# Moving the first loads, the narrowing of weights and the odd output tile of a fused FNet and gated-FFN kernel

## The chip, the cores and the metric

One NeuronCore of one Trainium2 chip runs the whole program. The metric is the device time of one execution in microseconds (us), given as the median of several runs with the lowest and highest beside it. A profile is one such execution seen by the hardware profiler; its span is some 2 us shorter than the time. The engines are called PE (TensorE matmul), PEld (its weight load), DVE (VectorE), ACT (ScalarE), POOL (GpSimd) and SP (SyncE, which here only issues transfers).

## The reference, cut to what matters

```python
X = np.fft.fft(np.fft.fft(x, axis=1), axis=2).real      # x: (8, 3136, 256) float32
h = np.maximum(X @ w_in, 0)                             # w_in: (256, 1024)  float64
c = sum(conv_w[k] * pad(h)[:, k:k + S] for k in range(3))  # three taps along the sequence
out = ((h / (1 + np.exp(-c))) @ w_out).astype(np.float32)  # w_out: (1024, 256) float64
```

The weights come as float64, so the kernel has to make float32 of their bit patterns itself, which is called narrowing here.

## The kernel before

For each of the 8 batches, DVE folds x (it uses the symmetries of the transform along the sequence, 14 operations per batch), PE multiplies the folds with tables of sines and cosines (the Fourier stage, nine *units* per batch), and then 32 *steps* follow: four *chunks* of the sequence times eight blocks of 128 features. In a step, PE makes two products (`pb`, `pa`), ACT copies one of them (`nb`), DVE adds and subtracts them with a clamp at zero (two "clamp adds", which make the front and the mirrored back part of `h`), ACT and DVE apply the three taps, ACT the sigmoid, POOL and DVE the gate, and three steps later PE multiplies the block with its part of `w_out`. The folds and units of the next batch are laid out as extra work into the steps of the batch before. Only batch 0 has to do its stage with nothing else to run.

The start: the order in which transfers are issued, and the tiny transfers of one partition each.

```python
w_cv.load(nc.scalar)
w_in[0].load(nc.scalar, 0)
w_in[0].load(nc.sync, 1)
for h in range(2):
    for f in load_ops(0, h, nc.sync):   # plain x, [five zero rows if h], 4 mirrored (indirect)
        f()
nc.scalar.dma_start(out=dm, in_=dft_dim[:, :, 0:2])
load_tables(1)                          # two big transfers and two table rows
for t in range(2):
    w_in[1].load(nc.sync, t)
load_tables(0)
...
w_cv.narrow(0, slice(0, P))
for t in range(2):
    w_in[0].narrow(t, slice(0, H))      # 7 DVE operations each
for f in fold_ops(0):
    f()
w_out.load(nc.sync)
taps()
blocks(0)                               # products of w_in's first half with dft_dim
for par in (1, 0):
    mend_tables(par, half)              # ACT: a halved row; for par 1 also two signed tables
```

The Fourier stage of batch 0, with a quarter of w_in's second half narrowed in each of four units, and what goes into the first steps:

```python
quarters = [(t, slice(i * H // 2, (i + 1) * H // 2)) for t in range(2) for i in range(2)]
for i, u in enumerate(us[j] for j in (0, 1, 4, 2, 3, 5, 6, 7, 8)):
    u.matmuls(0, 1)
    u.copy()
    ...
    u.fin()
    ...
    if i in (0, 1, 4, 5):
        w_in[1].narrow(*quarters.pop(0))
...
at(0, "pe", lambda: blocks(1))
for c in range(NF):
    at(c, "dve", lambda c=c: w_out.narrow(c, slice(0, D)))
```

The last product and the way out. A chunk has six tiles of 128 rows (one of them in a batch has 127), the last one seven, of which the seventh has 65 rows.

```python
osp = ctx.enter_context(tc.tile_pool(name="osp", bufs=3))
...
mm(pt[0:m, i % 2, :], gs[s][:, o:o + m], wout[:, f, :], ...)
if f == NF - 1 and (i % 2 or i == len(tiles) - 1):
    osb = osp.tile([P, 2, D], F32, name="os", tag="os")
    for j in range(i - i % 2, i + 1):
        nc.scalar.copy(out=osb[0:m, j % 2], in_=pt[0:m, j % 2])
        nc.sync.dma_start(out=rows[b * S + r:b * S + r + m, :], in_=osb[0:m, j % 2])
```

## Time and profile before

The time is 1279.84 us (1279.60 to 1280.65, three runs). I cut the span into the stretches that have different limits, by the times of the first clamp add of each batch:

| stretch | from to (us) | limit |
|---|---|---|
| loads, until PE starts the Fourier stage | 0 to 51.5 | transfers |
| stage of batch 0 | 51.5 to 73.3 | PE, then DVE |
| batch 0 | 73.3 to 248.0 | DVE in its first 19 steps |
| batches 1 to 5 | 248.0 to 992.3 | DVE and PE, in turns |
| batches 6 and 7 | 992.3 to 1276.1 | PE |
| last copy to the end | 1276.1 to 1279.0 | output transfers |

The page, the chain, SP's timeline and the busy times by stretch are shown in the prediction.

### The profile page before, as it was taken

To read this page: it belongs to the slowest core of one execution; us is meant where nothing else is said; L and a number is where in the kernel's file an instruction comes from. 1 tells how busy PE (TensorE), PEld (TensorE's weight loads), DVE (VectorE), ACT (ScalarE), POOL (GpSimd) and SP (SyncE) were. 2 spreads that over 40 slices of the span, in tenths; PEclk is the share of its full clock that TensorE was granted. 3 is DMA by queue.
4 is the path that set the end of the run, shared out by engine and by line. 5 is a ranking of instruction groups with operands and counts; after the bars stand their busy time and mean duration, and the time that the engine had idled before them with its cause. 6 is when DMAs were issued, how large, how long until landed. Compare 5 with 4: busy or idle time off the path is not lost.

```text
span 1279.0 us, 15442 instructions
## 1 busy us (share of the span) xinstructions
PE 1196.6 (94%) x4914; PEld 898.0 (70%) x4914; DVE 1145.5 (90%) x1689; ACT 884.4 (69%) x1823; POOL 398.5 (31%) x500
## 2 busy tenths in 40 slices
PE   2487899999999999999999999999999999999998
PEld 1355677677777777777677777777777777777776
DVE  7399999999999898998999888998999888898996
ACT  0254666677767777777777777777777777778885
POOL 4112532434424133241424224241322213222222
PEclk8688999999999999999999999999999999999999
DMA  7421321111212012020202103020010001000001
GB/s 198 122 76 33 94 76 47 55 52 52 68 59 76 11 43 76 25 78 25 89 13 63 41 25 101 26 78 5 22 50 26 27 26 44 32 17 15 26 29 44
DMA packets 47098, 66.04 MB, mean 52 GB/s; under 512 B 5600, under 2 KB 35196, under 8 KB 47016
## 3 DMA queue, kind: packets, MB, share of 16 engines
q1 hardware_dynamic: 41444, 51.39, 13.0%
q0 software_dynamic: 5120, 12.85, 3.6%
q10 hardware_dynamic: 452, 0.81, 0.2%
q8 instruction: 38, 0.62, 0.2%
q14 instruction: 44, 0.36, 0.1%
HBM read 39.24 MB, written 25.74 MB: 51 GB/s over the span
## 4 chain that ended last, share of the span: by engine, by line
PE 66%; DVE 16%; DMA 6%; issue 5%; ACT 5%; POOL 2%; SPq 1%; DVEq 0%; ACTq 0%; POOLq 0%
PE po L90 41%; PE pb L90 10%; PE pa L90 9%; PE pd L90 7%; DVE g L517 4%; DVE h L505 2%; DVE g L531 2%; DMA xh<-in_x_dram 2%; ACT nb L494 2%; DMA tab<-dft_seq_dram 2%; DMA out_dram<-os 2%; DVE xh L151 1%; ACT g L523 1%; DVE xh L162 1%; POOL xh L126 1%
## 5 line engine op out<-in xcount | busy, mean ns | idle before, releaser
L90 PE MATMUL po<-wout,g 128*128 128x256 f32 (+2 forms) x3200 | 742.4, 382 | 29.2 <-DVE g L531 25.7
L90 PEld LDWEIGHTS po<-wout,g 128*128 128x128 f32 (+2 forms) x3200 | 599.2, 188 | 193.9 <-DVE g L531 58.0
L517 DVE SCALAR_TENSOR_TENSOR g<-h,cw,g 128x770 f32<-128x770 f32 (+2 forms) x512 | 556.1, 1086 | 11.0 <-ACT g L511 1.5
L530 POOL TENSOR_TENSOR g<-g,h 128x385 f32<-128x385 f32 (+1 forms) x256 | 243.9, 954 | 760.6 <-ACT g L523 569.2
L523 ACT ACTIVATE g<-g 128x385 f32<-128x385 f32 (+3 forms) x512 | 244.0, 527 | 209.7 <-DVE g L517 209.5
L494 ACT ACTIVATE nb<-pb 128x386 f32<-128x386 f32 (+4 forms) x512 | 225.5, 493 | 98.0 <-PE pb L90 97.4
L505 DVE CUSTOM_DVE_ANT_0 h<-pa,nb 128x386 f32<-128x386 f32 (+4 forms) x512 | 264.8, 559 | 1.7 <-PE pa L90 1.6
L511 ACT ACTIVATE g<-h,cw 128x770 f32<-128x770 f32 (+2 forms) x256 | 243.5, 951 | 0.0
L90 PE MATMUL pb<-qt,G 127*128 127x386 f32 (+2 forms) x512 | 215.4, 501 | 4.8 <-ACT nb L494 4.8
L90 PE MATMUL pa<-pt,G 128*128 128x386 f32 (+2 forms) x512 | 213.3, 497 | 2.7 <-DVE pt L262 2.7
L531 DVE TENSOR_TENSOR g<-g,h 128x385 f32<-128x385 f32 (+2 forms) x256 | 154.6, 604 | 9.9 <-ACT g L523 9.9
L479 ACT ACTIVATE pa<-eb,ge 128x386 f32<-128x386 f32 (+2 forms) x256 | 153.6, 600 | 0.0
L90 PEld LDWEIGHTS pa<-pt,G 128*128 128x128 f32 x512 | 97.4, 190 | 77.1 <-issue 23.4
L90 PE MATMUL pd<-tab,w 99*128 99x196 f32 (+2 forms) x448 | 117.8, 374 | 0.0
L90 PEld LDWEIGHTS pb<-qt,G 127*128 127x128 f32 x512 | 94.2, 191 | 30.7 <-ACT nb L494 6.4
L126 POOL DMA_INDIRECT xh<-in_x_dram,idx x64 | 96.4, 1506 | 18.1 <-issue 12.0
L90 PEld LDWEIGHTS pd<-tab,w 99*128 99x128 f32 (+1 forms) x448 | 83.0, 190 | 13.6
L547 ACT COPY os<-po 128x256 f32<-128x256 f32 (+2 forms) x200 | 60.0, 395 | 23.3 <-DMA out_dram<-os 16.2
L151 DVE TENSOR_TENSOR xh<-xh 98x1020 f32<-98x1020 f32 (+1 forms) x32 | 44.9, 1409 | 0.0
L90 PE MATMUL po<-tab,w 98*128 98x196 f32 (+4 forms) x64 | 16.6, 420 | 26.3 <-ACT tab L215 15.6
L162 DVE TENSOR_TENSOR xh<-xh 98x1024 f32<-98x1024 f32 (+1 forms) x32 | 40.8, 1275 | 0.1
L90 PEld LDWEIGHTS po<-tab,w 98*128 98x128 f32 (+1 forms) x64 | 12.8, 215 | 29.6 <-ACT tab L215 16.1
(90 smaller groups left out, 324.5 us busy)
## 6 DMA issues: line engine op xcount, KB each, us to landing
out_dram<-os SPq DMA_DIRECT2D x184, 128.0 KB
xh<-in_x_dram SPq DMA_DIRECT2D x16, 784.0 KB
eb<-ed SPq DMA_DIRECT2D x16, 193.0 KB
tab<-dft_seq_dram SPq DMA_DIRECT2D x4, 601.8 KB
raw<-in_moe_w_out_dram SPq DMA_DIRECT2D x1, 2048.0 KB
eb<-ed SPq DMA_DIRECT2D x8, 209.0 KB
eb<-ed SPq DMA_DIRECT2D x8, 192.5 KB
raw<-in_moe_w_in_dram SPq DMA_DIRECT2D x3, 512.0 KB
```

The costliest lines, as they stand in the source:

```text
L90: nc.tensor.matmul(o, l, r, start=start, stop=stop, skip_group_check=True)
L126: nc.gpsimd.indirect_dma_start(out=xh[b, h][0:NP, 4 + m].rearrange("p q d -> p (q d)"), out_offset=None, in_=bass.AP(tensor=x.tensor, offs ...
L151: vt(a[:, :, :, 1:D], a[:, :, :, 1:D], r[:, :, :, D - 1:0:-1], op=ALU.add)
L479: act(pa[s][:, 0:n], eb[b, c], AF.Copy, scale=ge[:, f:f + 1])
L494: act(nb[s][:, i, cols], p[:, cols], AF.Copy, scale=-1.0 if i else 1.0)
L505: nc.vector._custom_dve(TENSOR_ADD_SAT, out=to, in0=a[:, cols], in1=c[:, i, cols], s0=BIG, s1=0.0)
L511: act(gs[s], hs[s][:, 0:n], AF.Copy, scale=cw[:, 0, s[2]:s[2] + 1])
L517: stt(out=g, in0=h[:, k:k + n], scalar=cw[:, k, f:f + 1], in1=g, op0=ALU.mult, op1=ALU.add)
L523: act(gs[s][:, c], gs[s][:, c], AF.Sigmoid)
L530: gt(g[:, m:n], g[:, m:n], h[:, m + 1:n + 1], op=ALU.mult)
L531: vt(g[:, 0:m], g[:, 0:m], h[:, 1:m + 1], op=ALU.mult)
L547: nc.scalar.copy(out=osb[0:m, j % 2], in_=pt[0:m, j % 2])
```

## The change

Its intent: (1) load x and the first tables ahead of the weights and in fewer transfers; (2) fold batch 0's x ahead of narrowing, and narrow and multiply w_in's first half inside the Fourier stage; (3) narrow w_in's second half in steps 0 and 1; (4) join the 64 odd rows of two batches to one full tile, so that two batches need 49 tiles of the last product and not 50; (5) spread the one-column "feature" products over four column tiles of PE. The core of the diff:

```diff
-            for s0, n, r, d in ((0, 4, 0, Q4), (4, 1, 0, Q4), (5, 1, 3, Q4), (6, 1, 2, Q4), (7, 1, 1, Q4)):
+            for s0, n, r in ((0, 4, 0), (4, 3, 1), (7, 1, 0)):          # zero rows
...
-        nc.sync.dma_start(out=tab[NP:KR, st, HQ - 1], in_=dft_seq[NP:KR, st, 1])
-        nc.sync.dma_start(out=tab[NP:KR, st, 0:HQ - 1], in_=dft_seq[NP:KR, st, 2:HQ + 1])
+    def load_row0():                                                    # one for both pairs
+        nc.sync.dma_start(out=tab[NP:KR, 0:4] ..., in_=...)
...
-    w_in[0].load(nc.scalar, 0)
-    w_in[0].load(nc.sync, 1)
-    for h in range(2):
-        for f in load_ops(0, h, nc.sync):
-            f()
     nc.scalar.dma_start(out=dm, in_=dft_dim[:, :, 0:2])
+    for f in load_ops(0, 0, nc.sync):
+        f()
+    ops = load_ops(0, 1, nc.sync)
+    for f in ops[0:1] + ops[2:]:
+        f()
     load_tables(1)
-    for t in range(2):
-        w_in[1].load(nc.sync, t)
-    load_tables(0)
+    load_row0()
+    ops[1]()                                                            # the zero rows
+    for i in range(2):
+        w_in[i].load(nc.sync)
+        if i == 0:
+            load_tables(0)
...
     w_cv.narrow(0, slice(0, P))
-    for t in range(2):
-        w_in[0].narrow(t, slice(0, H))
...
-    blocks(0)
...
+        if i < 2:
+            w_in[0].narrow(i, slice(0, H))                              # in the stage
-        if i in (0, 1, 4, 5):
-            w_in[1].narrow(*quarters.pop(0))
+        if i == 6:
+            blocks(0)
...
-    at(0, "pe", lambda: blocks(1))
+    for i in range(4):
+        at(i // 2, "dve", lambda i=i: w_in[1].narrow(i // 2, slice(...)))
+    at(1, "pe", lambda: blocks(1))
     for c in range(NF):
-        at(c, "dve", lambda c=c: w_out.narrow(c, slice(0, D)))
+        at(1 + c, "dve", lambda c=c: w_out.narrow(c, slice(0, D)))
...
-    end = 4
+    end = 5
-        stop = per * (b - 1) + max(26 - 8 * b, 2)
+        stop = per * (b - 1) + max(27 - 8 * b, 2)
...
+        if r.start < r.stop:                                            # gate, last chunk
+            vt(left[:, f, b % 2 * LEFT:(b % 2 + 1) * LEFT], g[:, r], h[:, r], op=ALU.mult)
...
+        if ch.last and b % 2:                                           # last product
+            tiles.append((left[:, f], [(i * LEFT, b - 1 + i, ch.rest[1], LEFT) for i in range(2)]))
...
-                        mms.append(product((slice(32 * c, 32 * c + 1), slice(j * n, (j + 1) * n)), ...))
+                        o = 32 * (2 * j + c)                            # feature products
+                        mms.append(product((slice(o, o + 1), slice(0, n)), ...))
```

Also the cuts of the chunks move by a column, the pool of copies gets four buffers, and `eb` four instead of five, with its last chunk loaded a little later.

## The prediction

> **What bounds the kernel now.** I read the page first, then the chain that ended last in order of time, the SP queue's timeline, the stretches of the first 50 us, and the busy time of each engine by step.
>
> From the page, part 1, the TensorE and VectorE rows of part 2, and the head of part 4:
>
> ```profile
> PE 1196.6 (94%) x4914; PEld 898.0 (70%) x4914; DVE 1145.5 (90%) x1689; ACT 884.4 (69%) x1823; POOL 398.5 (31%) x500
> ...
> PE   2487899999999999999999999999999999999998
> ...
> DVE  7399999999999898998999888998999888898996
> ...
> PE 66%; DVE 16%; DMA 6%; issue 5%; ACT 5%; POOL 2%; SPq 1%; DVEq 0%; ACTq 0%; POOLq 0%
> ```
>
> TensorE is full from about 180 us, but not in the first five slices, and the chain is 16% DVE and 6% DMA. So there are three regimes. The chain in order of time gives the first:
>
> ```profile
> 1.70 18.66 DMA xh<-in_x_dram
> ...
> 25.88 22.21 DMA tab<-dft_seq_dram
> 48.24 3.24 ACT tab L215 x4
> 51.52 2.34 PE po L90 x6
> ```
>
> (Start, length, piece.) The first Fourier products (51.5 us) wait for ACT to make two signed tables, and that waits for the second pair of table loads, landed at 48.2 us. Those were issued only at 25 us, because SP stood still before:
>
> ```profile
> 2.15 18.79 SPq L120 DMA_DIRECT2D xh<-in_x_dram  x5
> 20.98 1.67 SPq L202 DMA_DIRECT2D tab<-dft_seq_dram  x2
> ```
>
> The five tiny row transfers take SP 18.8 us: the third to fifth wait for the semaphores of w_in's half and of both big x loads. What that costs shows in the stretches (last column GB/s, before it the DMA share):
>
> ```profile
> 6.00:10.00 4.00, 0.44 (x2) 0.32 (x2) 0.00 (x0) 0.18 (x1) 3.02 (x4) 1.00 1.05 292
> ...
> 19.00:22.50 3.50, 3.50 (x8) 1.49 (x6) 3.43 (x6) 0.59 (x1) 0.68 (x1) 1.00 0.09 23
> 22.50:25.00 2.50, 1.73 (x17) 1.65 (x15) 2.47 (x4) 0.75 (x2) 0.64 (x2) 0.94 0.44 131
> ...
> 40.00:45.00 5.00, 0.00 (x0) 0.00 (x0) 0.00 (x0) 0.00 (x0) 0.00 (x0) 0.50 1.05 224
> ```
>
> 3.5 us with almost no traffic, then a weak 2.5 us. DVE is idle from 35.6 to 54.2 us.
>
> Second regime, batch 0's Fourier stage and the first 19 steps (a step: from one pair of L505 to the next). From 51.5 to 68.6 us TensorE has no gap (17.1 us). After the first L505 at 73.3 us, steps 1 to 18 are DVE without a gap: 7.2 us where a step carries narrowing (2.6) and a fold operation (1.2) besides its own 3.4, about 4.6 with the fold alone.
>
> Third, the steady state, batch 6 (992 to 1135 us) and batch 3 (546 to 695 us):
>
> ```profile
> 992.30:1135.10 142.80, 142.80 (x601) 109.36 (x600) 120.23 (x178) 108.81 (x227) 33.34 (x44) 1.00 0.09 29
> 545.50:694.90 149.40, 146.66 (x610) 110.45 (x608) 136.59 (x200) 109.45 (x227) 49.88 (x61) 1.00 0.16 49
> ```
>
> (Length, then busy PE, PEld, DVE, ACT, POOL.) Batch 6, which folds no later batch, is 100% TensorE. Batch 3, with 17.6 us of folds, takes 6.6 us more: there DVE and TensorE hold each other up step by step.
>
> [...] 22.5 to 25 us, with tables nearly alone, has share 0.44, which is 7/16. [...] The feature products (one output column) use two tiles now; in batch 0 their 16 instructions take 1.57 us [...].
>
> **Part 1, the start.** Removed: two tiny transfers per half-batch and two table-row transfers; the tables no longer queue behind them. In the changed program's instruction stream the SP order is x, x, first tables, rows, zero rows (two with waits), w_in half 0, second tables, w_in half 1, w_out. ACT's signed tables still wait for the second tables, so that landing stays the gate. [...] I take 39.5: **-8.7 us**. The zero rows now queue behind the first tables, so the second half's fold starts near 22 to 26 us and ends by 31 to 35, still earlier than the gate.
>
> **Part 2, batch 0's Fourier stage.** TensorE: 17.1 us as now, plus w_in half 0's products (G, ge), which ran at 18 to 24 us beside idle time and now stand inside the stage: at full clock 74.9 to 81.0 for the other half, 5.5 us. The feature products give back some 0.3. DVE: four quarters of w_in (4 x 2.6 = 10.4) leave, two halves (2 x 4.0 = 7.9) come in; it has 14 us of work under 22.3 of TensorE. So TensorE becomes the bound: 22.3 + 0.33 copy + 0.9 of sums, the first pa product at 23.4 us after the stage's start instead of 20.5: **+2.9 us**. First L505 near 67.5 us.
>
> **Part 3, w_in half 1 in steps 0 and 1.** Four quarters, 28 instructions of 0.28 to 0.43 us, 2.62 us a quarter: 10.5 us in a stretch where DVE is the chain and TensorE has slack (38.8 of 50.7 us busy). Nothing hides it: **+10.5 us**. Folds starting at step 5 instead of 4 move no sum.
>
> **Part 4, 49 tiles.** 25 tiles a batch become 24.5: 4 batches x 8 features x one 128x256 product of 0.432 us (12 instructions take 2.59) = 13.8 us less TensorE, all in the last chunk of even batches. DVE gets one 64-column product per feature in that chunk of every batch: [...] +0.10 us x 64 = 6.6 us. How much of 13.8 counts: batch 6 is pure TensorE, so 3.4. In batches 2 and 4 the 11 steps around the last chunk take 50.2 us; their TensorE work is 49.9, to become 46.4, and their DVE work is 47.3, to become 48.1: 2.1 at most, say 1.7 each. Batch 0: DVE work 50.9 of 54.4 us, say 1.0. Odd batches stay with TensorE: +0.5 for all. [...] Sum **-6.7 us**.
>
> **Part 5, features on four tiles, batches 1 to 7.** 16 instructions pitch at 82 ns; four tiles could give 41, but a one-column weight load takes 83 ns itself. I choose 0.3 us a batch: **-2 us**. More buffers for the copies and one fewer eb buffer: no wait in the trace to remove, 0.
>
> Sum: 1279.8 - 8.7 + 2.9 + 10.5 - 6.7 - 2.0 = 1275.8, **1276 us**.
>
> **Rivals.**
> (a) DVE becomes the bound everywhere: the change removes TensorE work and adds DVE work. For it: batch 3's DVE is 136.6 of 149.4 busy and the last chunk's steps show DVE at 99%. Against it: [...] batch 6 is clean. If it holds, part 4 is worth nothing or +4: 1282 to 1287.
> (b) The tables hide less or more. If the transfer rate near 40 us stays shared with w_out (it is issued earlier too[...]), landing could be 44: 1280. If seven engines alone run at their 153 GB/s of 30 to 34 us (about 22 KB/us each), landing could be 35: 1271.
> (c) The zero rows: queued behind tables, they could delay the second fold past the gate. They would have to land after 31 us[...]. It would cost 1 to 4 us.
> (d) The shifted narrowing is hidden, if steps 0 to 2 wait on TensorE anyhow: 1266. Against it: those steps are 94 to 96% DVE.
>
> **Range and chances.** The large terms carry +-3 (tables), +-2 (stage), +-1.5 (narrowing), +-4 (steady state), together about +-5.5, so 8 in 10 is some +-8, a little more on the slow side for (a): 1267 to 1286. Two per cent are 25.6 us: faster by that needs all of parts 1 and 4 with part 3 hidden (0.04); slower needs a new stall (0.02).
>
> **What would show it.** Right: second tables landed and ACT's tables begin between 37 and 42 us with no hole of traffic before 35; the first L505 near 67.5; steps 0 and 1 about 5 us longer each; the first L505 of batch 1 some 4 us later than the 248.0 of now; batches 2 and 4 about 2 us shorter, batch 6 about 3.5, odd ones unchanged. Wrong: the second fold ending after the tables' landing, batch 1 beginning earlier than 246, or the last chunk of even batches keeping its 37.9 us.

The forecast's sum is 1275.8. The working of part 1 came to a landing at 40.6 us; 39.5 was taken, and the -8.7 is 39.5 less 48.2. In part 4 the terms left come to -7.3, and a cut one of +0.6 makes the -6.7; its +0.10 us for the 64-column product was an estimate. Measured, that product takes 217 ns in the change and the other one 568 ns instead of 602 (384 columns instead of 416), which is +0.18. The seven engines are the share of 0.44 of 16: from 22.5 to 25 us the tables' packets, 6,288 bytes each, filled 7.0 engines' time. The 153 GB/s of (b) stood at a share of 0.57 and had w_in's packets in them (3.7 engines' time of the tables', 5.2 of w_in's), so they aren't the rate of seven engines alone.

## More of the kernel before

All tables lie in one tile, `tab = const.tile([P, 6, HQ, HE], ...)`; the signed tables are written into its planes 4 and 5.

One more view of the kernel before has to be seen, which the prediction didn't read: the groups by form (operation, output from input, the shape, how many; then busy us, mean ns of one; then the idle time of the engine before them and what ended it), here the copies from PSUM into the output buffers.

```profile
L547 ACT COPY os<-po 128x256 f32<-128x256 f32 x184 | 54.8, 395 | 7.1 <-PE po L90 6.9 <-issue 0.2
...
L547 ACT COPY os<-po 65x256 f32<-65x256 f32 x8 | 2.9, 368 | 16.2 <-DMA out_dram<-os 16.2
```

The eight copies of the lone 65-row tile, one per batch, wait 16.2 us in all for an output transfer to give its buffer back; the 184 others shown don't wait for one at all.

## The result and the profile after

The changed kernel takes 1278.96 us (1278.21 to 1279.89, four runs), the kernel before in the same rounds 1279.72 us (1279.44 to 1280.65, four runs). The ratio is 0.9993, with an interval of 0.9976 to 1.0010. Ratios in this document are the mean time of one kernel's fast runs over that of the other's of the same rounds, so they are not quite the ratios of the medians quoted beside them. The time lies inside the predicted range, 3 us above the predicted 1276.

The page after (busy us and share of the span, instructions; the PE and DVE rows of the 40 slices; the shares of the chain):

```profile
span 1277.4 us, 15522 instructions
...
PE 1178.4 (92%) x4850; PEld 887.1 (69%) x4850; DVE 1148.4 (90%) x1753; ACT 885.1 (69%) x1835; POOL 397.6 (31%) x500
...
PE   0567799999999999999999999999999999999997
...
DVE  4579998999999989899989989999999878899996
...
PE 64%; DVE 21%; issue 5%; DMA 4%; ACT 4%; POOL 1%; SPq 0%; DVEq 0%; ACTq 0%; POOLq 0%
```

PE's busy time fell by 18.2 us, but the span only by 1.6: the chain has 21% of DVE in it instead of 16, and PE's third and fifth slices are emptier than before (6 and 7 tenths instead of 8 each). The chain in order of time (start, length, piece) for the start:

```profile
20.65 21.98 DMA tab<-dft_seq_dram
...
42.79 3.24 ACT tab L220 x4
46.08 14.73 PE po L90 x62
60.81 3.43 PE pa L90 x8
64.24 4.60 PE po L90 x32
...
70.98 1.02 DVE h L525 x2
```

The same gate as before, ACT's signed tables behind the second tables' landing, now opens at 42.8 us instead of 48.2. The stage that follows takes 24.9 us from PE's first product to the first clamp add (46.08 to 70.98), against 21.8 (51.52 to 73.32). SP's timeline (start, length of issue, queue and line, what):

```profile
4.22 9.86 SPq L120 DMA_DIRECT2D xh<-in_x_dram  x3
19.28 0.42 SPq L426 DMA_DIRECT2D raw<-in_moe_w_in_dram  x1
19.75 1.67 SPq L202 DMA_DIRECT2D tab<-dft_seq_dram  x2
26.10 0.39 SPq L426 DMA_DIRECT2D raw<-in_moe_w_in_dram  x1
27.00 0.37 SPq L426 DMA_DIRECT2D raw<-in_moe_w_out_dram  x1
```

SP still stands behind the zero rows' waits until 14.1 us, waits another 5.2 us for a transfer of the tables, and issues w_in's first half only at 19.3. The second tables follow at 19.75, 5.2 us earlier than before (24.98 in its timeline). That is about the gain of the gate, 5.4: the change issues them earlier, but their way takes as long as before (22.0 us in the chain, 22.2 before). And w_out now follows them at 27.0 us; before, it was issued at 34.7. The stretches of the start (length; busy us of PE, PEld, DVE, ACT, POOL; clock, DMA share, GB/s):

```profile
19.00:22.50 3.50, 0.00 (x0) 0.00 (x0) 3.47 (x4) 0.00 (x0) 1.32 (x2) 1.00 0.80 235
22.50:25.00 2.50, 0.00 (x0) 0.00 (x0) 2.43 (x5) 0.00 (x0) 1.05 (x2) 1.00 0.95 214
...
34.00:40.00 6.00, 0.00 (x0) 0.00 (x0) 2.22 (x4) 0.00 (x0) 2.71 (x3) 1.00 1.05 222
```

The hole of 19 to 25 us (23 and 131 GB/s before) is full. Yet from 34 to 40 us the share is 1.05, all 16 engines, where tables nearly alone had 0.44, seven of 16 (22.5 to 25 us before): something runs beside them. (The 1.00 of the clock column measures nothing here: the first clock record of this trace is at 52.29 us, and that of before at 21.27.)

By batch, from its first clamp add to that of the next (batch 7 to the last output copy), in us:

| batch | 0 | 1 | 2 | 3 | 4 | 5 | 6 | 7 |
|---|---|---|---|---|---|---|---|---|
| before | 174.7 | 147.6 | 149.9 | 149.3 | 149.5 | 147.9 | 142.8 | 141.0 |
| after | 182.3 | 150.6 | 149.7 | 147.2 | 148.4 | 145.1 | 141.8 | 136.0 |

The first clamp add comes 2.3 us earlier, batches 0 and 1 lose 10.5 us, batches 2 to 7 gain 12.3, and the end after the last copy takes 5.4 us instead of 2.9. The stretches of batches 6 and 3 show that the regimes are the same as before:

```profile
994.20:1136.00 141.80, 141.80 (x597) 109.24 (x597) 120.58 (x186) 109.24 (x230) 32.15 (x44) 1.00 0.09 30
553.50:700.70 147.20, 144.76 (x602) 109.70 (x602) 136.54 (x207) 109.44 (x228) 49.87 (x61) 1.00 0.16 50
```

Batch 6 is still nothing but PE, and in batch 3 the distance between the span and PE's busy time went from 2.7 to 2.4 us.

Most of the gain of batch 7 lies in one step. Before, step 227 (chunk 0 of batch 7) took 8.11 us; after, it takes 3.98. The timeline of before at that place:

```profile
1153.07 0.37 ACT L547 COPY os<-po 65x256 f32<-65x256 f32 x1 [3.32 <-DMA out_dram<-os]
...
1154.30 0.91 DVE L531 TENSOR_TENSOR g<-g,h 128x384 f32<-128x384 f32 x1 [4.13 <-ACT g L523]
...
1155.08 0.92 PE L90 MATMUL pb<-qt,G 127*128 127x385 f32 x2 [1.70 <-ACT nb L494]
```

The number in brackets is the idle time before the instruction, and behind it what ended that. The copy of the lone tile waits 3.32 us for an output transfer. On ACT the sigmoid of DVE's gate and the copy that PE needs start behind it, at 1153.34 and 1154.17 us, and DVE idles for 4.13 us and PE for 1.70. The cause: the last chunk has seven tiles, two to a buffer, so it takes four buffers at one time from a pool of three. After the change, even batches have six tiles there; the same group reads

```profile
L577 ACT COPY os<-po 128x256 f32<-128x256 f32 x196 | 58.1, 397 | 10.6 <-PE po L90 6.2 <-DMA out_dram<-os 4.3
```

The wait for output transfers went from 16.2 us to 4.3. Nothing in the prediction's part 4 counts that. But the wait isn't all of batch 7's 5.0 us: where it alone is taken away (e5 below), step 227 takes 4.68 us, three of the next four steps grow by 0.4 to 0.5 us each, and the batch gains 2.4. The other 2.7 are what separates e2b, which has the wait removed but all the products, from the change (138.6 and 136.0 us).

The feature products of batch 0, before and after (how many; duration ns least, median, most; first to last start):

```profile
L90 PE MATMUL po<-tab,ea x16: 333/336/339, 57.2 to 58.5; 98*1 98x197 f32 x6, 98*1 98x196 f32 x6, 99*1 99x197 f32 x2, 99*1 99x196 f32 x2
```

```profile
L90 PE MATMUL po<-tab,ea x16: 333/336/347, 53.0 to 53.5; 98*1 98x197 f32 x6, 98*1 98x196 f32 x6, 99*1 99x197 f32 x2, 99*1 99x196 f32 x2
```

One product lasts as long as before, but 16 of them start within some 0.5 us instead of 1.3: four column tiles do work side by side.

### The profile page after: what moved, and what is told of

Same layout as the page of the kernel before. It is cut to its first block, busy times and chain, and to the rows that moved or that the text cites. A ratio compares the mean times of both kernels' runs of the same rounds, so it can differ in the third digit from the quotient of the medians.

```text
span 1277.4 us, 15522 instructions
## 1 busy us (share of the span) xinstructions
PE 1178.4 (92%) x4850; PEld 887.1 (69%) x4850; DVE 1148.4 (90%) x1753; ACT 885.1 (69%) x1835; POOL 397.6 (31%) x500
## 4 chain that ended last, share of the span: by engine, by line
PE 64%; DVE 21%; issue 5%; DMA 4%; ACT 4%; POOL 1%; SPq 0%; DVEq 0%; ACTq 0%; POOLq 0%
PE po L90 40%; PE pb L90 9%; PE pa L90 9%; PE pd L90 6%; DVE g L537 6%; DVE h L525 4%; DMA tab<-dft_seq_dram 3%; DVE g L558 3%; ACT nb L514 2%; DVE xh L151 1%; DVE xh L162 1%; DVE w L178 1%; ACT g L550 1%; DVE w L179 1%; DVE xh L167 0%
## 5 line engine op out<-in xcount | busy, mean ns | idle before, releaser
L90 PE MATMUL po<-wout,g 128*128 128x256 f32 x3072 | 716.3, 383 | 37.5 <-DVE g L558 34.0
L90 PEld LDWEIGHTS po<-wout,g 128*128 128x128 f32 x3072 | 579.7, 191 | 200.7 <-DVE g L558 78.4
L537 DVE SCALAR_TENSOR_TENSOR g<-h,cw,g 128x770 f32<-128x770 f32 (+1 forms) x512 | 555.2, 1084 | 10.6 <-ACT g L531 1.5
L550 ACT ACTIVATE g<-g 128x385 f32<-128x385 f32 (+2 forms) x512 | 244.4, 528 | 223.2 <-DVE g L537 223.0
L514 ACT ACTIVATE nb<-pb 128x386 f32<-128x386 f32 (+3 forms) x512 | 225.6, 494 | 83.5 <-PE pb L90 82.6
L525 DVE CUSTOM_DVE_ANT_0 h<-pa,nb 128x386 f32<-128x386 f32 (+3 forms) x512 | 264.8, 558 | 0.9 <-PE pa L90 0.9
L531 ACT ACTIVATE g<-h,cw 128x770 f32<-128x770 f32 (+1 forms) x256 | 243.6, 951 | 0.2 <-DVE h L525 0.2
L90 PE MATMUL pb<-qt,G 127*128 127x387 f32 (+2 forms) x512 | 214.3, 499 | 2.6 <-ACT nb L514 2.4
L90 PE MATMUL pa<-pt,G 128*128 128x387 f32 (+2 forms) x512 | 212.6, 496 | 0.4 <-DVE pt L267 0.4
L499 ACT ACTIVATE pa<-eb,ge 128x387 f32<-128x387 f32 (+2 forms) x256 | 154.0, 602 | 3.1 <-DVE h L525 3.1
L126 POOL DMA_INDIRECT xh<-in_x_dram,idx x64 | 95.9, 1498 | 18.1 <-issue 12.3
L151 DVE TENSOR_TENSOR xh<-xh 98x1020 f32<-98x1020 f32 (+1 forms) x32 | 44.4, 1391 | 12.6 <-DMA xh<-in_x_dram,idx 10.3
```

Source lines behind the costliest of these rows:

```text
L90: nc.tensor.matmul(o, l, r, start=start, stop=stop, skip_group_check=True)
L126: nc.gpsimd.indirect_dma_start(out=xh[b, h][0:NP, 7 - m].rearrange("p q d -> p (q d)"), out_offset=None, in_=bass.AP(tensor=x.tensor, offs ...
L151: vt(a[:, :, :, 1:D], a[:, :, :, 1:D], r[:, :, :, D - 1:0:-1], op=ALU.add)
L499: act(pa[s][:, 0:n], eb[b, c], AF.Copy, scale=ge[:, f:f + 1])
L514: act(nb[s][:, i, cols], p[:, cols], AF.Copy, scale=-1.0 if i else 1.0)
L525: nc.vector._custom_dve(TENSOR_ADD_SAT, out=to, in0=a[:, cols], in1=c[:, i, cols], s0=BIG, s1=0.0)
```

## The experiments

Twelve kernels ran, each with runs of the kernel before. All gave the right result. Their differences to before of the same rounds are what I compare. None is called faster or slower at the 2% mark, so the intervals have to tell them apart.

| kernel | us, median (lowest to highest; runs) | before, same rounds | difference | ratio and interval |
|---|---|---|---|---|
| the change | 1278.96 (1278.21 to 1279.89; 4) | 1279.72 | -0.76 | 0.9993 (0.9976 to 1.0010) |
| e1_quarters_in_stage | 1274.49 (1273.96 to 1275.04; 4) | 1279.91 | -5.42 | 0.9956 (0.9940 to 0.9973) |
| e2_25_tiles | 1286.65 (1284.45 to 1287.97; 4) | 1279.91 | +6.74 | 1.0056 (1.0039 to 1.0073) |
| e3_feature_two_tiles | 1281.02 (1280.01 to 1281.41; 4) | 1279.91 | +1.11 | 1.0008 (0.9991 to 1.0025) |
| e4_tables_apart | 1267.60 (1266.46 to 1268.82; 4) | 1279.91 | -12.31 | 0.9901 (0.9884 to 0.9917) |
| e5_before_lone_buffer | 1274.90 (1273.94 to 1275.35; 4) | 1279.72 | -4.82 | 0.9960 (0.9945 to 0.9975) |
| e2b_25_tiles_lone | 1282.41 (1281.39 to 1282.91; 4) | 1279.72 | +2.69 | 1.0018 (1.0003 to 1.0034) |
| e6_win0_first | 1273.36 (1272.81 to 1275.78; 4) | 1279.72 | -6.36 | 0.9955 (0.9940 to 0.9971) |
| e8_all | 1257.87 (1257.02 to 1258.97; 5) | 1279.72 | -21.85 | 0.9829 (0.9816 to 0.9843) |
| e7_wout_later | 1275.36 (1274.51 to 1277.45; 4) | 1279.54 | -4.18 | 0.9973 (0.9958 to 0.9988) |
| e9_shift_undone | 1278.20 (1276.42 to 1278.46; 5) | 1279.54 | -1.34 | 0.9989 (0.9976 to 1.0003) |
| e10_all_unshifted | 1257.18 (1255.86 to 1257.67; 5) | 1279.54 | -22.36 | 0.9824 (0.9811 to 0.9838) |
| e11_all_wout_later | 1256.45 (1256.13 to 1256.79; 4) | 1279.54 | -23.09 | 0.9822 (0.9807 to 0.9837) |

### Part 3 undone

The second half of w_in is narrowed in the stage again, a quarter in each of four units.

```diff
+        if 2 <= i < 6:
+            w_in[1].narrow((i - 2) // 2, slice(i % 2 * H // 2, (i % 2 + 1) * H // 2))
...
-    for i in range(4):
-        at(i // 2, "dve", lambda i=i: w_in[1].narrow(...))
```

> The changed kernel with part 3 undone: the four quarters of w_in's second half are narrowed in batch 0's Fourier stage again (behind the third to sixth unit) and no longer in steps 0 and 1. Theory (DVE is the chain in the first steps, so the 10.5 us are paid in full; in the stage TensorE hides most of them): the first L525 about 2 us later than the 71.0 of the changed kernel, steps 0 to 8 together 10 us shorter, the first L525 of batch 1 near 245.5 instead of 253.3, time 1271 (1269 to 1273). Rival (the narrowing in steps 0 and 1 is hidden behind TensorE or is made up by the end of batch 0): batch 1 begins at 253 or later, time 1279 to 1282.

Batch 0 takes 172.5 us instead of 182.3: the narrowing costs 9.8 us in the steps. The stage, from PE's first product (46.76) to the first clamp add (75.90), takes 29.1 us instead of 24.9, so 4.2 come back there; batch 2 gives back another 1.2 (149.7 to 150.9). The time is 4.7 us better than that of the change (5.42 less 0.76). Part 3 is therefore a loss: it moves 9.8 us to where nothing hides them and saves 4.2. The direction and the 10 us in the steps came as expected, but the time missed the expected 1269 to 1273, because the first clamp add came 4.9 us later and not 2: the stage hides less of the quarters than I thought.

### Part 4 undone

Chunks, cuts, gate and last product are those of before (25 tiles per batch), and the rest is that of the change.

```diff
-            tiles.append((left[:, f], [(i * LEFT, b - 1 + i, ch.rest[1], LEFT) for i in range(2)]))
...
+            mm(pt[0:m, i % 2, :], gs[s][:, o:o + m], wout[:, f, :], ...)
```

> The changed kernel with part 4 undone: 25 tiles of the last product per batch again, a 65-row tile at the end of each, no 64-column product on DVE. Theory (the saved TensorE time counts where TensorE is behind: after the last chunk of even batches and in batch 6): batches 6 and 7 together 4 to 5.5 us longer, batches 2 to 5 together 2 to 4 longer, time 1286 (1284 to 1289). Rival (a) of the prediction (DVE is the bound everywhere): the removed 64-column products pay instead, 1275 to 1279.

The time rises by 7.5 us against the change (6.74 and 0.76), so part 4 is worth about that, near the predicted 6.7. This run alone can't say by what: it brings back both PE's products and the fourth buffer of the last chunk. Nor does the gain lie where it was expected: batches 6 and 7 are together 3.4 us longer than in the change, not 4 to 5.5, and batches 2 to 5 together 5.0, not 2 to 4.

### Part 5's feature products undone

Two column tiles again, as in the kernel before.

```diff
-            for i in range(2):
-                for j, qs in enumerate(((3, 1), (2, 0))):
+            for j, qs in enumerate(((3, 1), (2, 0))):
+                for q in qs:
...
-                        o = 32 * (2 * j + c)
+                            (slice(32 * c, 32 * c + 1), slice(j * n, (j + 1) * n)), ...
```

> The changed kernel with part 5 undone: the feature products on two column tiles. In the changed kernel's trace their 16 instructions start within 0.5 us (53.0 to 53.5) against 1.3 us (57.2 to 58.5) before. Theory (each batch's stage is on TensorE's path): 0.7 us a batch, time +3 to +5.5: 1282 to 1284. Rival (the feature unit's step is held by something else): 1279, within 0.5.

The time rises by 1.9 us (1.11 and 0.76), and the sum of the eight batches in the profile by 1.95. That is less than the theory's 3 to 5.5 and more than the rival's 0.5. The two intervals overlap, so the sign rests on the agreement of time and profile, and the batches don't share it evenly: batches 0, 5 and 6 are 0.6 to 0.7 us longer, batches 3, 4 and 7 not at all.

### The signed tables off the second tables' landing

ACT's signed tables are made of the first pair alone. In the change ACT sits idle for 15.65 us ahead of them, until a transfer of the tables ends. The theory is that they wait for the second pair because all tables lie in one tile. Here each pair has its own tile, and the units that use the first pair and the signed tables come first.

```diff
-    tab = const.tile([P, 6, HQ, HE], F32, name="tab")
+    tabs = [const.tile([P, 2, HQ, HE], F32, name="tab%d" % i) for i in range(3)]
...
-    for i, u in enumerate(us[j] for j in (0, 1, 4, 2, 3, 5, 6, 7, 8)):
+    for i, u in enumerate(us[j] for j in (0, 1, 5, 6, 4, 2, 3, 7, 8)):
```

> The changed kernel with the tables in three tiles instead of one (first pair, second pair, signed), so that ACT's signed tables no longer wait for the second pair's load, and with the four odd units ahead in batch 0's stage, since they need only the first pair. Theory (the landing of the second tables at 42.7 us gates the stage only by that false dependency; the odd products are ready once the second fold's odd features are, at 32.4 us): first products near 33 us instead of 46, the first L525 near 57 (55 to 61) instead of 71.0, time 1265 (1262 to 1269). Rival (DVE, with 8 us of narrowing in the stage, or the even units' tables hold it anyhow): first L525 at 65 to 70, time 1273 to 1278.

The first clamp add comes at 60.06 us instead of 70.98, and the time is 11.6 us better than the change's (12.31 less 0.76), so all of it is kept. The chain no longer has the tables in it:

```profile
12.91 13.91 DMA xh<-in_x_dram
...
28.18 1.21 DVE xh L151
...
60.06 1.02 DVE h L525 x2
```

ACT's four operations for the signed tables begin at 26.9 us, 16 us earlier than in the change. The gate of the prediction's first part was real in time but false as a dependency: the data were there all that time before. The run makes two edits at once, the tiles and the order of the units, so the 11.6 us belong to both together.

### The buffer wait by itself, in the kernel before

The lone tile gets a buffer of its own of 1 KB per partition. No run tried a fourth full buffer of 2 KB.

```diff
+    olp = ctx.enter_context(tc.tile_pool(name="olp", bufs=1))
...
-                osb = osp.tile([P, 2, D], F32, name="os", tag="os")
+                osb = (osp.tile([P, 2, D], F32, name="os", tag="os") if i % 2
+                       else olp.tile([P, 1, D], F32, name="ol", tag="ol"))
```

> The kernel before, with one small output buffer of its own for the lone 25th tile, so that ACT's fourth copy of a batch's last chunk no longer waits for an output transfer (16.2 us of ACT idle over 8 batches before, 4.3 in the changed kernel). Theory ([...]this wait holds back the sigmoid behind it and with it DVE and TensorE: in step 227 it takes 3.3 us, and the step 8.1 instead of about 5): 1 to 2 us a batch in batches 1 to 5, 3 in batch 7, time 1273 (1270 to 1276). Rival (ACT has 30% idle time, the wait is off the path): 1279.5 to 1280.

```profile
L549 ACT COPY ol<-po 65x256 f32<-65x256 f32 x8 | 3.0, 381 | 0.0
```

The wait of 16.2 us is gone, and the kernel before becomes 4.8 us faster, more than the whole change gave. It shows as 2.4 us in batch 7 (141.0 to 138.6) and 0.7 to 1.0 us in each of batches 2 to 5 (1 to 2 were expected). Only about 5 of the 16.2 us were on the path.

### The same buffer in the kernel without part 4

The edit is that of e5, made in e2.

> The changed kernel with 25 tiles a batch, as before, but with the small output buffer for the lone tile. Theory (of the 7.7 us that part 4 is worth, the larger part is the vanished wait for an output buffer in even batches): 1281 to 1283. Rival (it is the TensorE time, as the prediction had it): 1286, as with 25 tiles alone.

It is 4.0 us faster than e2 (6.74 less 2.69), and the sum of its batches in the profile is 3.9 less (1206.95 against 1210.84). The sum of the change's batches is another 6.0 less (1200.98). So part 4 has two gains of their own causes: some 4 us of a vanished wait for a buffer, and what PE no longer does, some 6 us in the batches. Of these 6 only 3.4 reach the time (2.69 and 0.76). In the two profiles the rest goes where the batches don't count: the change's first clamp add comes 0.9 us later than e2b's (70.98 and 70.10) although the signed tables begin together (42.79 and 42.82), because the stage's first 14 products took 6.95 us and not 6.08, a scatter that the account of part 2 comes back to; and its end takes 1.8 us longer (5.4 and 3.6). From the last copy to the end of the span, the four kernels with 25 tiles (before, e2, e2b, e5) took 2.9 to 4.2 us, and seven with 49 tiles per two batches (the change, e1, e3, e4, e6, e7, e9) 4.1 to 5.4; their means differ by 1.1. The time is within the expected 1281 to 1283; that the wait is the larger part of part 4 holds for the time (4.0 of 7.5) and not for the batches. That the two 64-row transfers of the last tile, issued one after the other, are the cause is argued and not tested.

### w_in's first half in front again

Part 2 undone on top of the change, keeping its fewer transfers.

```diff
+    w_in[0].load(nc.scalar, 0)
+    w_in[0].load(nc.sync, 1)
...
     w_cv.narrow(0, slice(0, P))
+    for t in range(2):
+        w_in[0].narrow(t, slice(0, H))
...
+    blocks(0)
```

> The changed kernel with w_in's first half loaded, narrowed and multiplied first again, as before; the fewer transfers, the order of the rest and all later parts stay. Theory (the folds can't use the place ahead of the narrowing, since they wait for x: in the changed kernel DVE sits idle 12.6 us ahead of fold adds and the second fold ends at 36.2 us, as against 35.6 before; so the narrowing costs nothing there, and its products leave the stage): second fold ends by 38, signed tables at 42 to 44 us, first L525 at 65 to 67 instead of 71.0, time 1274 (1272 to 1276). Rival (w_in ahead of x pushes the folds behind the tables): fold ends after 43, first L525 at 70, 1278.

The second fold ends later, at 38.4 us, but before the signed tables begin (41.48), and the first clamp add comes at 64.09 instead of 70.98. The time is 5.6 us better (6.36 less 0.76). Of the 6.9 us, 1.3 are an earlier landing (41.48 instead of 42.79), and the rest is the stage, out of which PE's products of that half have gone: in the change they take it from 60.65 to 65.78, 5.1 us. Folding ahead of narrowing gains nothing here, because DVE waits for x's transfers anyway; its timeline in the change has these waits at the folds' first operations:

```profile
12.76 1.22 DVE L151 TENSOR_TENSOR xh<-xh 98x1020 f32<-98x1020 f32 x1 [6.76 <-DMA xh<-in_x_dram,idx]
17.53 1.22 DVE L151 TENSOR_TENSOR xh<-xh 98x1020 f32<-98x1020 f32 x1 [3.55 <-DMA xh<-in_x_dram,idx]
...
27.45 2.35 DVE L151 TENSOR_TENSOR xh<-xh 99x1020 f32<-99x1020 f32 x2 [2.25 <-DMA xh<-in_x_dram]
```

Together 12.6 us of idle DVE, into which the 7.9 us of narrowing fit again in e6.

### All of these together

Tables apart, w_in's first half in front, the quarters in the stage, and the buffer for the lone tile.

> All that the runs so far point to, on the changed kernel: tables in three tiles with the odd units first, w_in's first half loaded, narrowed and multiplied first, the quarters of its second half in the Fourier stage, a small output buffer for the lone 49th tile. Theory (the effects add up): first L525 at 54 to 57, steps 0 to 8 10 us shorter, time 1253 (1249 to 1257). Rival (the stage becomes DVE's with 10.4 us of narrowing in it and eats the table gain): first L525 at 60, 1258 to 1262.

The kernel takes 1257.87 us, 21.1 better than the change, although the single gains of e4, e6, e1 and e5 would sum to about 27. It is the rival's case (first clamp add at 60), and the time lies just below the rival's 1258 to 1262. The profile says where they overlap: the first clamp add comes at 60.42, no earlier than in e4 alone, and batch 0 takes 172.7 us as in e1. The stretch of the stage reads

```profile
41.00:59.00 18.00, 12.41 (x68) 9.31 (x67) 16.29 (x42) 5.90 (x14) 6.91 (x11) 0.85 0.42 135
```

DVE is busy 16.3 of 18 us, PE 12.4: now the stage is bound by DVE, which has the quarters to narrow in it, and what e6 gave alone doesn't show in it; no run takes the quarters alone out of e8 again to confirm this. Batches 1 to 7 are only 0.8 us shorter than in the change (1017.9 against 1018.7), so the lone buffer adds little once the even batches have no seventh tile.

### w_out's load out of the tables' way

The changed kernel with w_out's load issued behind the second unit of batch 0's stage.

```diff
-    w_out.load(nc.sync)
...
             row()
+            w_out.load(nc.sync)
```

> The changed kernel, with w_out's 2 MB load issued behind the second Fourier unit of batch 0 instead of right behind w_in's second half. Theory (the second tables landed at 42.7 us and not at 39.5 because w_out's transfers ran beside them from 28 us on and held their seven engines to some 14.5 KB per us each, against 22 to 23 alone): the 172 KB per engine from 27.5 us then take about 8 to 10 us less the w_in half that is still mixed in; the signed tables begin near 37 us instead of 42.8, the first clamp add comes near 65 to 66 instead of 71.0, and as nothing else moves the time is about 1273 to 1274. Rival (the tables' own descriptors, or w_in's second half ahead of them in the same queue, set the pace): landing stays at 42 to 43 and the time at 1279. A second way to fail: w_out now lands late for its narrowing at step 1 or delays batch 1's x, which would show as steps 1 to 9 longer by a few us.

```profile
34.00:40.00 6.00, 0.00 (x0) 0.00 (x0) 2.16 (x4) 0.04 (x1) 2.70 (x3) 1.00 0.41 152
```

```profile
39.95 3.24 ACT tab L220 x4
...
68.12 1.02 DVE h L525 x2
```

Between 34 and 40 us the share falls from 1.05 to 0.41, about 7 of 16 engines, and these carry 152 GB/s, 22 per engine (152/7), where all 16 carried 222 together, 14 per engine. The packets in the two traces agree: one of the tables, 6,288 bytes, took 443 ns on the mean beside w_out's and takes 270 without them. In the change the tables' packets filled 6.9 engines' time there and w_out's, of 2,048 bytes, 9.7. So here a load was slowed by one that ran beside it; by what means stays open. The signed tables begin at 39.95 and the first clamp add comes at 68.12, 2.9 us earlier, and the time is 3.4 us better than the change's (4.18 less 0.76). The direction of the theory holds and the rival's unchanged landing doesn't, but my size of it was wrong: 5 to 6 us expected, about 3 seen (its 14.5 KB per us and engine beside w_out and 22 to 23 alone were measured as 14 and 22). The landing also scatters from kernel to kernel: e2, e2b, e3, e9 and e1, which issue their first loads as the change does, began the signed tables at 41.3 to 43.5 us; e7's 39.95, a single profile, is 1.4 below the lowest of these. Steps 1 to 8 are unchanged, so the late w_out disturbs nothing.

### The shift of the schedule undone

```diff
-        stop = per * (b - 1) + max(27 - 8 * b, 2)
+        stop = per * (b - 1) + max((27 if b == 1 else 26) - 8 * b, 2)
```

> The changed kernel with the fold and Fourier schedule of batches 2 to 7 put back by one step to where the kernel before has it (only batch 1's fold keeps its start at step 5 and its end at 19). Theory (the +3.0 us of batch 1 against before, which every variant so far shows, come from that shift): batch 1 falls from 150.5 to about 147.6 to 148.5 and the time to about 1276 to 1277. Rival (batch 1's sum is longer because of the odd batch's forty-ninth tile and the cuts, or only because work moved across the border between batches 0 and 1): batch 1 stays within 0.7 of 150.5 or batch 2 gives back what it gains, and the time stays at 1279 within 1.

Batch 1 falls to 149.1 us and batch 2 to 149.1, but batch 0 rises to 183.4; the sum of the three is 1.0 less. The time is 0.6 us better, which the intervals (0.9976 to 1.0003 and 0.9976 to 1.0010) don't tell from nothing. The rival holds for the time. Half of batch 1's extra 3.0 us came from the shift (150.6 to 149.1), and 1.1 of that is work that goes back over the border into batch 0; where the other half comes from isn't shown. That the border moved is also what e1 suggests: its batches 0 and 1 together take 323.1 us, against 322.3 before.

### The combination with the shift undone, and then with w_out late

The edits are those of e9 and of e7, made in e8 one after the other.

> e8_all with the schedule put back by one step as in e9. Theory: the gain of e9, if there is one (2 to 3 us), is kept, as it lies in other batches than the gains of e8: 1255 to 1256. Rival (the shift costs nothing): 1257.9 as e8_all within 1.

> e10_all_unshifted with w_out's load late as in e7. Theory (in e8 and e10 the stage no longer waits for the second tables, which stand in their own tile and are used late, and it is VectorE that sets its end): the transfer that e7 takes away is hidden, so the first clamp add stays at 60.4 within 1 us and the time is that of e10 within 1.5. Rival (the folds or w_in's narrowing in this stage still wait for transfers that w_out slows down): the first clamp add comes 2 us or more earlier and the time falls by as much.

e10 is 0.5 us better than e8 (22.36 less 21.85) and e11 another 0.7 (23.09 less 22.36), both within the scatter of the runs, so the rival of e10 holds; in e11 the first clamp add stays at 59.57 (59.62 in e10). So w_out's transfers are hidden where the tables no longer gate the stage, as its theory said. e10 and e11 are the best kernels, 1.8% faster than before by the ratio, with the whole interval below 0.984.

## Why the prediction was right, and where it wasn't

The total was right to 3 us. Its steps, in order:

| step of the prediction | predicted us | shown us | from |
|---|---|---|---|
| 1: second tables land earlier | -8.7 | -5.4 | 48.2 to 42.8 in the chains |
| 2: stage of batch 0 | +2.9 | +3.1 | 21.8 to 24.9 |
| 3: narrowing in steps 0 and 1 | +10.5 | +9.8 | batch 0, change and e1 |
| 4: 49 tiles | -6.7 | -7.5 (products -3.4, buffer -4.0) | e2, e2b |
| 5: feature products | -2.0 | -1.9 | e3 |
| shift of the schedule | 0 | +0.6, unsure | e9 |
| sum | -4.0 | -1.3 | measured: -0.8 |

**Part 1 is the step that was mis-sized.** The prediction's working came to a landing at 40.6 us and it took 39.5, so 1.1 of the 3.3 us missed were given away there. The working is cut, as it shared the loads out among the engines in a way that no trace shows; its 40.6 was the author's estimate. And it assumed that w_out would not slow the tables more than in the mean of before, where w_out ran only from 34.7 us on; now it is issued at 27.0. e7 shows that it does: without w_out beside them the signed tables begin at 39.95 and not at 42.79. The prediction's own rival (b) had this case, "landing could be 44: 1280", and the result is 42.8 and 1279. It also took the gate itself for given; e4 shows that it was worth 11.6 us more, because the wait came from a shared tile and not from shared data (with the units put in an order that uses this).

**Parts 2 and 3 held to 1 us.** The stage became PE's, and nothing hid the narrowing, though steps 0 and 1 grew by 2.6 and 4.9 us and not by 5 each. But part 2's working held partly by luck. It read 74.9 to 81.0 us as 5.5 us of products, which is 6.1 and begins with another product (the granted clock is 0.50 from 72.47 and 1.00 from 75.89 to 86.13 us); in the change they take 5.1 (60.65 to 65.78). Its 22.3 + 0.33 + 0.9 is 23.5 and not 23.4. And it didn't see that PE starts the stage slower for longer. The first 14 products, before and after (PE's timeline):

```profile
51.52 5.80 PE L90 MATMUL po<-tab,w 99*128 99x196 f32 x14 [15.55 <-ACT tab L215]
```

```profile
46.08 6.95 PE L90 MATMUL po<-tab,w 99*128 99x196 f32 x14 [12.40 <-ACT tab L220]
```

In both a product of 392 columns starts every 653 ns at first and every 330 later, but the faster pace comes at 55.4 us before, 3.9 us into the stage, and at 52.3 after, 6.2 us into it. The clock records change there too: before, the granted clock is 0.50 from 24.69 to 55.41 us and then 1.00; after, the first record, of 1.00, is at 52.29, and the trace says nothing of the time ahead of it. That costs about 1.2 us, most of which smaller products hid: 5.1 instead of 5.5, and 0.7 saved by the feature products instead of 0.3 (1.57 to 0.89 us in the same timelines). It is no property of the change: the same 14 products take 5.66 to 6.95 us in the six kernels whose stage begins alike (e9, e2, e2b, e3, e7 and the change), and what sets the moment isn't shown. The direction in which the work was moved was the wrong one for the time: before, w_in's first half was narrowed and multiplied ahead of the stage, in time that e6 shows to be free, and e6 gets 5.6 us by putting it back.

**Part 4 was right in sum by luck: two errors cancel.** The products gave 6.0 us in the batches of the profile, but only 3.4 in the time, half of the 6.7. The prediction placed them in the last chunk of the even batches. They came in the chunk after: between e2b and the change, chunk 0 of batches 3 and 5 went from 35.7 to 34.3 us and that of batch 7 from 32.6 to 29.4, while the last chunk of batches 2, 4 and 6 stayed (39.1, 37.9 and 36.4 us in e2b, 39.3, 38.1 and 36.3 in the change), which is one of the prediction's own signs of being wrong. That the last products run three steps late explains a part of this; that PE goes into the next batch less far behind, where DVE was the limit, explains the rest and is argued only. "Batches 2 and 4 about 2 us shorter, odd ones unchanged" is wrong for the same reason: 0.2 and 1.1 in the even ones, 2.1 and 2.9 in batches 3 and 5; and batch 6 gained 1.0 where 3.4 were counted, the rest coming in batch 7. What the prediction didn't see at all is the wait for an output buffer: 3.9 us in the profiles and 4.0 in the times, and 4.8 in e5, where nothing else was changed. It was readable beforehand, in the two lines by form shown above, and the working looked at busy times only. In the profiles about 1 us of the gain is lost at the end of the program, for a cause that isn't tested.

**Part 5** held: four tiles do start a product every 0.04 us (some 0.5 us for 16), and the chosen 0.3 us a batch sums to what e3 shows, though not spread evenly and at the edge of the noise.

**The rivals.** (a), DVE bound everywhere, falls: the products were worth 3.4 us in the time, where it had nothing or a loss. (c), zero rows delaying the second fold past the gate, didn't come: that fold ends at 36.2 us. (d), hidden narrowing, falls by e1.

What stays open: why the landing of the tables scatters by 2 us between kernels with the same order of loads, why PE's pace rises earlier in some than in others, and what exactly the end of the program waits for.

## What to carry to other kernels

Before moving loads or work to open a gate earlier, ask whether the instruction at the gate needs the data it waits for: here separate tiles for the tables, with the units that need only the first ones in front, were worth 11.6 us, where reordering the transfers opened the gate 5.4 us earlier. Read the copies out of PSUM by form: one small group with all the idle time in front of it can mean a pool one buffer short, and a buffer of 1 KB per partition was worth more than the whole change. Move work into idle time of its engine, and measure each part of a change alone, since this one hid some 10 us of narrowing in batch 0's first steps behind gains of the same size.
